# Eight small copies per head pair, from ScalarE to GpSimd

## The chip, the cores and the metric
The kernel runs on one core of a Trainium2 chip. Five engines run their own instruction queues in order and meet through semaphores: TensorE (PE in the profile; its weight loads are PEld), VectorE (DVE), ScalarE (ACT), GpSimd (POOL) and SyncE (SP), which here issues most of the DMAs. The metric is the device time of one execution in microseconds. Before, three runs gave a median of 1098.16 us (1097.16 to 1098.83).

## The reference
Two blocks follow each other. The first is an attention whose scores count only where query and key fall into the same of 64 hash buckets; the second mixes by a Fourier transform, normalizes, and applies a two-layer perceptron. Sizes: batch 4, 8 heads, sequence 768, head size 64, so the model width is 512 and the hidden width 2048.

```python
q_bits = (np.einsum('bhsd,dk->bhsk', q, proj) > 0)        # 6 bits: a bucket per row
mask = q_bucket[:, :, :, None] == k_bucket[:, :, None, :]
scores = np.where(mask, scale * q @ k^T, -1e9)
attn = exp(scores - max); attn = attn / (sum(attn) + 1e-9)
x = (attn @ v) laid out as (B, S, H*D)
mixed = np.real(fft(fft(x, axis=1), axis=2))
u = x + mixed
un = (u - mean(u)) / sqrt(var(u) + 1e-6)
out = u + np.maximum(un @ w_ch1, 0.0) @ w_ch2
```

The copies in question belong to the division by `sum(attn)`.

## The kernel before
**Order of the work.** The 32 heads are taken two at a time: 16 pairs, four for each of the four batches. `attention(b)` (L972) goes through the pairs of a batch; for each pair it makes the transposed scores in six chunks of 128 keys (`scores`, L894), their exponentials on ScalarE (`weights`, L905), the bucket mask on VectorE (`weigh`, L919, two of them a chunk; in the first five pairs the mask is folded into the scores by an extra product, L886), the running sum of the chunks on VectorE (L1007), and the products with the values on TensorE (`values`, L930). Between chunks the generator yields, and the main loop (from L1536) takes steps of `mix(b - 1)` there: the Fourier products of the batch before (`fold` L1072, L1122, L1151, L1165), then its perceptron `mlp7`, whose first layer is written as seven products for each block of hidden units (`inner`, L1426, evacuated by L1448 to L1477) and whose second layer likewise (`outer7`, L1306, evacuated by L1318 to L1358). The statistics for the normalization run in `spread` (L1183 to L1188), the last two instructions of it on GpSimd.

In the first batch, ScalarE and VectorE also turn the raw 64-bit weights into floats (`narrow`, L639 to L655): `weights1` during the attention of batch 0, `weights2` during that of batch 1. The loads of `weights2` (L693) are issued from GpSimd's queue, two raw buffers deep; so are the stores of the first three batches (L1060). L576, L568 and L562 load q, k and v from SP's queue, L768 transposes q and k, L750 takes their norms on ScalarE.

**What sets the order.** The instructions up to the end of batch 0's attention stand in the program's own order on TensorE, VectorE, ScalarE and GpSimd (`tc.manual_schedule`, with L1528 to L1535 at its end). From there on, a scheduler in the compiler's front end places the instructions of each engine by its own estimate of their costs; so a change of one instruction's engine can move others.

**The changed place.** `scale` (L936) finishes a pair. ScalarE moves the two accumulated halves out of PSUM (L941, L944). TensorE sums the exponentials over the partitions by products with ones, each of the four quarters of 32 partitions receiving the sums of one (half, head) (L949). VectorE transposes that in 32 x 32 blocks (L956), so that the 384 sums of a quarter stand as 32 partitions x 12 columns, adds a small constant (L958) and takes the reciprocal, `rc` (L959). There the generator yields once. Then eight copies of 32 partitions x 12 columns lay `rc` out as `rr`, each quarter of `rc` on two quarters of partitions (L965); VectorE transposes `rr` back, each column repeated 32 times (L966), and multiplies the pair's result by it (L970). `rr` has two buffers, `rt` one.

The second transpose waits for all eight copies, and all eight wait for the reciprocal. The other neighbours that the prediction speaks of: L669 and L672, averages of weight rows at the end of batch 0; L839, L843 and L849, the bucket numbers of the later pairs; L1082 to L1100 (`fold`); L1272 to L1275 and L1277, sums of second-layer weights; L1177 and L1178 (`across`), transposes of the normalization's input; L1405 to L1411, sums for `mlp7`; L1325, L1336 and L1339, ScalarE's copies out of PSUM in `outer7`; L1326 and L1334, sums on VectorE there. PSUM tiles of these parts come from pools of two banks, so a product can start only when the evacuation two tiles back is done.

Of the kernel before, what the change touches and what calls it, by code (L numbers as in the profile page):

```python
# [485 lines left out]
def _main(  # L486
# [13 lines left out]
    nc = tc.nc  # L500
# [13 lines left out]
    def wt(shape, dtype, tag, name, bufs=2):  # L514
        return work.tile(shape, dtype, tag=tag, name=name, bufs=bufs)
# [4 lines left out]
    def pt(shape, name):  # L520

        turn[0] += 1
        if roomy[0] and turn[0] % 2:
            if turn[0] % 4 == 1:
                return ps_o.tile(shape, F32, tag="o", name=name)
            return ps_sc.tile(shape, F32, tag="sc", name=name)
        return ps_1.tile(shape, F32, tag="ps", name=name)
# [408 lines left out]
    def scale(n, oos, sums):  # L936


        x = xs[n // NPAIR][:, n % NPAIR]
        vs = wt([P, 1], F32, "vs", f"vs{n}")  # L940
        nc.scalar.copy(vs, oos[0][:, HALF : HALF + 1])  # L941
        halves = [x[:, g * HALF : (g + 1) * HALF] for g in range(2)]
        for g, xg in enumerate(halves):
            nc.scalar.activation(xg, oos[g][:, 0:HALF], AF.Identity, bias=vs)  # L944

        ps = pt([P, HALF], f"sum{n}")
        for i, part in enumerate(sums):
            for j in range(4):
                nc.tensor.matmul(  # L949
                    ps[32 * j : 32 * j + 32, :], ones, part[:, j // 2, j % 2],  # L950
                    start=(i == 0), stop=(i == len(sums) - 1),
                )


        rt = wt([P, S], F32, "rt", f"rt{n}", 1)
        nc.vector.transpose(rt[:, 0:HALF], ps)  # L956
        rc = wt([P, HALF // 32], F32, "rc", f"rc{n}")
        nc.vector.tensor_scalar(rc, rt[:, 0:HALF:32], S * EPS, None, op0=ALU.add)  # L958
        nc.vector.reciprocal(rc, rc)  # L959
        yield  # L960
        rr = wt([P, 2, HALF // 32], F32, "rr", f"rr{n}")
        for g in range(2):
            for i in range(4):
                j = 2 * g + i // 2
                nc.scalar.copy(rr[32 * i : 32 * i + 32, g], rc[32 * j : 32 * j + 32])  # L965
        nc.vector.transpose(  # L966
            rt.rearrange("p (j i) -> p j i", i=32),
            rr.rearrange("p g j -> p (g j)")[:, :, None].broadcast_to([P, S // 32, 32]),
        )
        nc.vector.tensor_tensor(x, x, rt, op=ALU.mult)  # L970

    def attention(b):  # L972
# [3 lines left out]
        def finish():  # L976
            n, c, pk, oos, sums = pending.pop(0)
            with behind() if n >= NPAIR and t is not None else nullcontext():
                values(n, c, pk, oos)
            if c == NT - 1:  # L980
                scales.append(scale(n, oos, sums))
                next(scales[-1])
# [647 lines left out]
```

## Time and profile before
| | |
|---|---|
| median of three runs | 1098.16 us |
| the profiled execution | 1095.54 us, its span 1093.6 us |
| TensorE busy | 1034.4 us (95%) |
| VectorE busy | 788.6 us (72%) |
| ScalarE busy | 499.2 us (46%) |
| GpSimd busy | 58.3 us (5%), 132 instructions |
| TensorE's granted clock, mean | 0.994 |
| DMA | 103.14 MB, 94 GB/s on average |

The span is the time between the first and the last record of one execution. A line of the profile gives start and length in microseconds, the engine, the line of the kernel, the operation, output and inputs by the program's names with their shapes, and a count; in brackets stands how long the engine had been idle before it and what ended that. A group's line gives least, median and greatest duration in nanoseconds. TensorE idles little, and nearly all of its gaps lie in the first 340 us and around 420 to 490 and 680 to 750; the rest of the span it is busy for 19 to 20 of every 20 us.

### The profile page before, as it was taken

What the parts mean: (1) busy time and instruction counts of PE and PEld (TensorE: products, weight loads), DVE (VectorE), ACT (ScalarE), POOL (GpSimd) and SP (SyncE); (2) the same over time, 40 slices, a digit from 0 to 9 for tenths busy, and PEclk for the clock granted to TensorE, in tenths of its full rate; (3) what the DMA queues carried; (4) which work ended last, traced back from release to release, by engine and by line L of the source; (5) the groups of instructions that cost most, each with busy time, mean ns of one, the idle gap of its engine ahead of it and who ended that gap; (6) DMA issues with size and microseconds to landing.
All of it is one profiled execution on the core that took longest, in us unless ns stands there. A gap on an engine that the chain in (4) does not pass through costs nothing.

```text
span 1093.6 us, 14135 instructions
## 1 busy us (share of the span) xinstructions
PE 1034.4 (95%) x4933; PEld 633.6 (58%) x4933; DVE 788.6 (72%) x1336; ACT 499.2 (46%) x1055; POOL 58.3 (5%) x132
## 2 busy tenths in 40 slices
PE   7989897999989999999999999999999999999996
PEld 3333354446744676545664576645675579768675
DVE  5899968868599978694857786876765875644353
ACT  6987556653276324354325424354415522340420
POOL 0000000002000020010000011001000002100000
PEclk9999999999999999999999999999999999999998
DMA  9755352440056162223063224213123205122401
GB/s 233 216 97 126 63 145 67 164 149 11 20 155 207 43 206 40 54 57 84 15 181 85 63 63 159 44 36 91 25 82 113 76 20 173 54 82 84 129 20 42
DMA packets 175711, 103.14 MB, mean 94 GB/s; under 512 B 129552, under 2 KB 162960, under 8 KB 175632
## 3 DMA queue, kind: packets, MB, share of 16 engines
q1 hardware_dynamic: 169840, 88.65, 30.2%
q0 software_dynamic: 4224, 13.11, 3.8%
q8 instruction: 41, 0.67, 0.2%
q10 hardware_dynamic: 1568, 0.39, 0.2%
q14 instruction: 38, 0.31, 0.1%
HBM read 81.14 MB, written 20.97 MB: 93 GB/s over the span
## 4 chain that ended last, share of the span: by engine, by line
PE 57%; DVE 16%; ACT 4%; issue 2%; DMA 2%; DVEq 0%; ACTq 0%
PE o L1306 23%; PE h_p L1426 18%; PE oo L930 5%; PE sc L894 5%; DVE pk L919 5%; DVE acc L1007 3%; PE cs L1122 2%; DMA zraw<-in_moe_w_ch_dram 2%; PE A L1151 1%; PE B L1151 1%; ACT pk L905 1%; ACT rr L965 1%; PE bits L825 1%; DVE x L1165 1%; DVE h L1464 0%
## 5 line engine op out<-in xcount | busy, mean ns | idle before, releaser
L1306 PE MATMUL o<-w,h 128*128 128x256 f32 x1152 | 258.5, 381 | 2.0 <-DVE w L1318 0.8
L1306 PEld LDWEIGHTS o<-w,h 128*128 128x128 f32 x1152 | 216.8, 190 | 41.8 <-issue 3.5
L905 ACT ACTIVATE pk<-sc 128x768 f32<-128x768 f32 x192 | 146.8, 808 | 93.4 <-PE oo L930 30.6
L1426 PE MATMUL h_p<-x,w 128*128 128x384 f32 x448 | 162.4, 492 | 2.2 <-ACT h L1448 1.7
L894 PE MATMUL sc<-qt,kt 64*128 64x384 f32 x768 | 153.5, 502 | 5.9 <-ACT pk L905 5.6
L930 PE MATMUL oo<-pk,vn 128*64 128x385 f32 (+1 forms) x768 | 149.2, 499 | 6.8 <-DVE pk L919 4.4
L919 DVE SCALAR_TENSOR_TENSOR pk<-qb,kb,pk 128x768 f32<-128x768 bf16 x132 | 129.1, 1010 | 34.3 <-ACT pk L905 34.0
L1426 PEld LDWEIGHTS h_p<-x,w 128*128 128x128 f32 x448 | 82.5, 190 | 67.1 <-issue 6.5
L1007 DVE TENSOR_TENSOR acc<-acc,pk 128x1536 f32<-128x1536 f32 (+1 forms) x72 | 105.7, 1482 | 5.7 <-ACT pk L905 5.1
L1426 PE MATMUL h_p<-w 128*128 128x384 f32 x288 | 106.4, 492 | 3.5 <-ACT w L1463 2.3
L930 PEld LDWEIGHTS oo<-pk,vn 128*64 128x64 f32 x768 | 50.7, 136 | 95.0 <-issue 73.3
L894 PEld LDWEIGHTS sc<-qt,kt 64*128 64x128 f32 x768 | 66.4, 186 | 56.8 <-ACT pk L905 19.1
L1426 PEld LDWEIGHTS h_p<-w 128*128 128x128 f32 x288 | 53.0, 190 | 45.5 <-ACT w L1475 5.1
L1318 DVE SCALAR_TENSOR_TENSOR w<-o,rs,w 128x256 f32<-128x256 f32 x56 | 26.7, 477 | 42.4 <-PE o L1306 42.4
L1336 ACT COPY tq<-o 128x256 f32<-128x256 f32 x24 | 8.9, 372 | 101.8 <-PE o L1306 101.8
L1306 PE MATMUL o<-w 128*128 128x256 f32 x176 | 42.0, 381 | 0.3 <-DVE w L1318 0.3
L1459 DVE TENSOR_TENSOR h<-h 128x384 f32<-128x384 f32 x32 | 17.7, 552 | 29.5 <-ACT h L1458 29.5
L1452 DVE TENSOR_TENSOR h<-h 128x384 f32<-128x384 f32 x32 | 17.7, 553 | 26.8 <-ACT h L1451 26.7
L1306 PEld LDWEIGHTS o<-w 128*128 128x128 f32 x176 | 33.0, 190 | 6.8 <-issue 1.1
L1060 POOL DMA_DIRECT2D out_dram<-w x30 | 16.4, 548 | 376.4 <-ACT tq L1336 146.2
L1325 ACT COPY tq<-o 128x256 f32<-128x256 f32 x24 | 8.9, 369 | 58.4 <-PE o L1306 58.3
L1122 PE MATMUL cs<-ch,z 128*128 128x128 f32 (+3 forms) x192 | 31.7, 317 | 3.0 <-DVE bt L829 1.9
(170 smaller groups left out, 1311.4 us busy)
## 6 DMA issues: line engine op xcount, KB each, us to landing
w<-ad SPq DMA_DIRECT2D x168, 128.0 KB, 2.0
w<-bd SPq DMA_DIRECT2D x42, 512.0 KB, 4.5
zraw<-in_moe_w_ch_dram POOLq DMA_DIRECT2D x16, 512.0 KB, 4.0
bd<-w SPq DMA_DIRECT2D x14, 512.0 KB, 4.2
vn<-in_v_dram SPq DMA_DIRECT2D x32, 192.0 KB, 3.4
qn<-in_q_dram SPq DMA_DIRECT2D x120, 48.0 KB, 2.3
kn<-in_k_dram SPq DMA_DIRECT2D x60, 96.0 KB, 3.1
zraw<-in_moe_w_ch_dram SPq DMA_DIRECT2D x8, 512.0 KB, 5.9
```

The lines of the kernel that those rows point to most:

```text
L894: last[0] = nc.tensor.matmul(ps[:, h, 0:HALF], kt[rows, ks], qt[rows, qs], start=kb is not None, stop=True,)
L905: nc.scalar.activation(pk[:, g, :, 0:HALF], ps[:, :, 0:HALF], AF.Exp, scale=SCALE)
L919: nc.vector.scalar_tensor_tensor(w, qb[:, h].rearrange("p (g s) -> p g s", g=2), kb[:, h, c : c + 1], w, op0=ALU.is_equal, op1=ALU.mult,)
L930: oo = nc.tensor.matmul(oos[g][h * D : (h + 1) * D, 0:w], nat["v", n][:, (2 * c + h) * D : (2 * c + h + 1) * D], pk[:, g, h, 0:w], start=( ...
L1007: nc.vector.tensor_tensor(acc[:, g], (first if c == 1 else acc)[:, g], new[:, g], op=ALU.add,)
L1122: nc.tensor.matmul(ps[:, pc + 2 * lo : pc + 2 * hi - 1 : 2], z[:, cp, pc, par, t * P : (t + 1) * P], ch[:, cp, pc, lo:hi], start=(cp == 0) ...
L1151: nc.tensor.matmul(ps[:, cols], F[:, par, k, t, j * P : (j + 1) * P], sq[:, t, k, cols], start=(t == 0), stop=(t == 1),)
L1306: nc.tensor.matmul(ps, a[:, r], right7[i][:, r], start=start and r == 0, stop=r == HF // 2 - 1, skip_group_check=not start,)
L1318: nc.vector.scalar_tensor_tensor(t[:, cols], src, r, t[:, cols], op0=ALU.mult, op1=ALU.add)
L1426: nc.tensor.matmul(ps, left[:, k], right[i][:, k], start=start and k == 0, stop=k == 1, skip_group_check=not start,)
L1452: nc.vector.tensor_tensor(c21, c12, c21, op=ALU.add)
L1459: nc.vector.tensor_tensor(c22, c21, c22, op=ALU.add)
```

## The change
The eight copies of L965 are issued on GpSimd instead of ScalarE. Shapes, sources, destinations and the instructions before and behind them in the program stay.

```diff
         for g in range(2):
             for i in range(4):
                 j = 2 * g + i // 2
-                nc.scalar.copy(rr[32 * i : 32 * i + 32, g], rc[32 * j : 32 * j + 32])
+                nc.gpsimd.tensor_copy(rr[32 * i : 32 * i + 32, g], rc[32 * j : 32 * j + 32])
         nc.vector.transpose(
             rt.rearrange("p (j i) -> p j i", i=32),
             rr.rearrange("p g j -> p (g j)")[:, :, None].broadcast_to([P, S // 32, 32]),
         )
```

## The prediction
> **What bounds the kernel now.** I read the page's busy shares first, then the group of the eight copies with who waits for it, then TensorE's own idle gaps, then the order of time around each of the 16 pairs. The pairs are numbered 0 to 15 in the order of their copies.
>
> ```profile
> PE 1034.4 (95%) x4933; PEld 633.6 (58%) x4933; DVE 788.6 (72%) x1336; ACT 499.2 (46%) x1055; POOL 58.3 (5%) x132
> ```
> TensorE is busy 1034.4 of 1093.6 us. Only its 59 us of gaps can shrink, and what grows them costs time.
>
> ```profile
> L965 ACT COPY rr<-rc x128: 183/198/202, 42.9 to 898.0; 32x12 f32<-32x12 f32 x128
> ...
>   DVE rt L966: 11.4, 13
> ```
> The copies' line: 128 copies of about 198 ns. VectorE's transpose (L966) stood idle 13 times, 11.4 us in all, until they were done.
>
> ```profile
> 20.00:100.00 80.00, 73.29 (x496) 28.82 (x492) 74.17 (x124) 72.57 (x146) 0.11 (x1) 1.00 0.65 171
> ```
> The stretch with pairs 0 to 2 (columns: PE, PEld, DVE, ACT, POOL busy): ScalarE works 72.57 of 80 us, and VectorE is fuller still, 74.17.
>
> ```profile
> 47.66 0.34 PE L886 MATMUL sc<-qkb 64*128 64x384 bf16 x2 [1.59 <-ACT pk L905]
> 75.48 0.34 PE L886 MATMUL sc<-qkb 64*128 64x384 bf16 x2 [1.94 <-ACT pk L905]
> 324.45 1.56 PE L1426 MATMUL h_p<-x,w 128*128 128x384 f32 x4 [1.53 <-ACT h L1448]
> 385.15 1.99 PE L1306 MATMUL o<-w,h 128*128 128x256 f32 x8 [0.74 <-ACT tq L1325]
> 466.81 1.56 PE L1426 MATMUL h_p<-w 128*128 128x384 f32 x4 [1.14 <-ACT w L1463]
> ```
> TensorE's waits for ScalarE just behind copies (pairs 0, 1, 6, 7, 8): in brackets the idle time and whom it waited for.
>
> **What GpSimd charges.** Before has no GpSimd copy, so its price is bounded.
>
> ```profile
> 1.45 0.12 POOL L603 MEMSET ones<- 128x32 f32 x1
> 1.50 0.10 POOL L605 MEMSET mhalf<- 128x1 f32 x1
> 478.77 0.22 POOL L1187 TENSOR_SCALAR rs<-mv 128x1 f32<-128x1 f32 x1 [68.45 <-DVE mv L1185]
> 951.76 0.51 POOL L1187 TENSOR_SCALAR rs<-mv 128x1 f32<-128x1 f32 x2
> ```
> Fills that read nothing start 0.05 us apart and overlap. An instruction that reads and writes SBUF takes 0.22 alone; two in a row take 0.51, so the second starts about 0.29 after the first. Eight copies then last between 0.22 + 7 x 0.05 = 0.57 and 8 x 0.29 = 2.3 us. I take 8 x 0.22 = 1.76: L1187 is nearest in kind (small, one input read) but each L1187 also waits for a semaphore, which six of the eight copies don't. To this comes 0.09 us from VectorE's end to GpSimd's start (478.68 to 478.77). So 1.85 us against ScalarE's 1.70 (0.05 and 1.65): the new route is slightly longer where VectorE stands idle for it.
>
> Where VectorE does not stand idle, another row matters.
>
> ```profile
> 260.48 1.76 DVE L1007 TENSOR_TENSOR acc<-acc,pk 128x1536 f32<-128x1536 f32 x1
> 260.63 1.69 POOL L1187 TENSOR_SCALAR rs<-mv 128x1 f32<-128x1 f32 x1 [1.07 <-DVE mv L1185]
> ```
> The 0.22 us instruction took 1.69, until a VectorE instruction with two inputs from SBUF ended. A copy that falls beside such a one is held.
>
> The row leaves VectorE unharmed: at 258.11 its two-input L919, behind a held L1187, took the usual 1.01. [...]
>
> **The change, part by part.** It takes 128 copies, 16 x 1.65 = 26 us, off ScalarE, and puts them on GpSimd. No DMA and no byte is added. The built order of the changed kernel shows that instructions move too: VectorE reaches L966 earlier, ahead of two of L1165 (pair 4), L1272, L639, L1273 and L643 (pair 6) and L1326 (pairs 7, 11, 15), which then stand behind the wait.
>
> Queues. SP keeps its transfers; in the changed order only a few neighbours swap (ad writes and reads with q and k loads), which I cost at nothing since the copies issue none; if one that TensorE needs is late, the price is about a landing, 2.0 us (median of w<-ad). On GpSimd the copies stand behind whatever was issued before them. By the times of before, that is done in time for all but two: pair 4 starts at 179.54 behind a raw-weight load issued at 179.01 (ScalarE began at 180.14), pair 7 at 383.23 behind a store (ScalarE: 383.03). What is queued behind them: in pair 5 the L1187 chain, needed only from about 256, and in pair 6 a load that matters.
>
> - **Pairs 0 to 2.** ScalarE is freed of 1.65 three times. TensorE's gaps that this can close are 1.59 and 1.94 (1.65 of it), 3.2 together; the third has no gap behind it. Against it, VectorE runs two-input work between the reciprocal and L966, and one copy slips in at each boundary: nine boundaries in pair 0 (no wait), five in pairs 1 and 2, so three copies are left, 0.66 us of wait against 0.28 and 0. As VectorE is the fuller engine, I take half the gaps less half the new waits: -1.1 (from -3.2 to 0).
> - **Pair 3.** L669 no longer queues behind copies and a 1.10 gap before L672 shrinks; L966 comes 0.15 later and VectorE sets the next gap (1.05 at 130.93). -0.4 (-1.1 to +0.7).
> - **Pair 4.** The 2.63 gap at 184.43 goes, because the exponential is issued ahead of a conversion that waits for a load. But the second L1165 of B ends at 181.3 + 0.9 + 0.43 + 0.87 + 0.43 = 183.9, not 180.54, and the transposes (L1177) wait for it. -0.3 (-1.2 to +0.5).
> - **Pair 5.** ScalarE frees a 0.98 gap, VectorE's second L919 ends within 0.1 of before. 0 (-1.0 to +0.6).
> - **Pair 6.** The dear one.
>
> ```profile
> 319.67 1.67 ACT L965 COPY rr<-rc 32x12 f32<-32x12 f32 x8 [0.21 <-DVE rc L959]
> 320.46 0.53 POOL L693 DMA_DIRECT2D zraw<-in_moe_w_ch_dram  x1 [7.58 <-DVE w L1272]
> 321.57 0.97 DVE L966 STREAM_TRANSPOSE rt<-rr 128x768 f32<-128x768 f32 x1
> 325.00 0.68 ACT L647 ACTIVATE zraw<-zraw 128x512 int32<-128x512 uint32 x1 [0.59 <-DMA zraw<-in_moe_w_ch_dram]
> 325.57 0.47 ACT L1451 COPY h<-h_p 128x384 f32<-128x384 f32 x1
> ```
> Here GpSimd's load, VectorE's L966 and ScalarE's next conversion stand in the order of time. Copies end at 319.92 + 1.76 = 321.7 (the first is held to 319.92 by L652). The load behind them goes out 1.3 later than 320.46, so L647 starts near 326.2, and L1451, behind it on ScalarE, at 327.4 instead of 325.57. TensorE's next product needs the bank that L1451 empties. The gap of 1.53 closes and a larger one opens behind it: +1.8 (+0.6 to +2.4).
> - **Pair 7.** L1325 is freed, the 0.74 gap goes. But copies end at 383.3 + 1.76 = 385.06, and L966, L1326, L970 and L1318 end at 387.8 instead of 387.1; TensorE waits for that bank. +0.7 (-0.4 to +1.3).
> - **Pairs 8 and 12.** The gaps of 1.14 and 1.13 go, but the chain runs through VectorE (L966 466.29 to L1007 479.25 without a break): +0.12 for the copies, up to +0.5 for a statistic (L1183) put ahead of two masks. +0.3 each (-1.15 to +0.85).
> - **Pairs 11 and 15.** L1326 falls behind L966, so the L1318 that empties a bank ends 0.6 later, and TensorE starts right after it now (645.08, then 645.13). +0.6 each (0 to +1.2).
> - **Pairs 9, 10, 13, 14.** L1007 holds the copies for 1.7 us and L966 comes about 1.3 later. TensorE has 20.00 of 20 us of work in 520 to 540 and 780 to 800, and 19.95 in 580 to 600 and 840 to 860: 0; without that cover about 1.4 each, 5.6.
>
> Sum: -1.1 - 0.4 - 0.3 + 0 + 1.8 + 0.7 + 0.6 + 1.2 = +2.5 us. The profiled execution took 1095.54 (span 1093.6 and 1.9 around it), so 1098.0. The median of the runs, 1098.16, lies 2.6 above it; there +2.5 gives 1100.7.
>
> **Rivals.**
> 1. *The copies overlap as the fills do (0.66 us from reciprocal to transpose).* For it: six of eight wait for nothing. Against it: fills read no SBUF, and L1187 shows no overlap. All the low ends: -3.2 - 1.1 - 1.2 - 1.0 + 0.6 - 0.4 - 2.3 + 0 = -8.6, 1089.6. It is faster from about 0.15 us per copy on. This is the rival on the other side.
> 2. *The copies are dear (0.29 each) and nothing is gained in pairs 0 to 2.* High ends: 0 + 0.7 + 0.5 + 0.6 + 2.4 + 1.3 + 1.7 + 2.4 = +9.6, 1107.8; with the cover of pairs 9, 10, 13, 14 gone, 1113.4.
> 3. *Gains and losses cancel:* the weight stretch passes all of -3.2 on while the later terms stay: +0.4, 1098.6.
> That the change moves nothing is excluded: the built order has all 128 copies on GpSimd.
>
> **How the numbers follow.** About 0.2% (2.2 us) is what a measurement here tells from no change. The forecast's case has 40% (slower in 23 of them, same 12, faster 5, as the reordering adds a few us either way), rival 1 24% (faster 20, same 4), rival 2 24% (slower 22, same 2), rival 3 12% (same 8, faster 3, slower 1). Faster 0.28, same 0.26, slower 0.46. The range 1091 to 1110 leaves out the far ends of rivals 1 and 2. The forecast's own range is 1098 to 1104.
>
> **What would show it.** ScalarE's busy time falls to about 473, GpSimd's rises by 20 or more. A copy on GpSimd near 0.22 us and eight in about 1.8; L966's waits, 11.4 now, at 20 or more; the load of pair 6 issued over 1 us after the reciprocal; gaps at 47.66 and 75.48 smaller. I am wrong if eight copies last about 1 us, if VectorE's instructions lengthen beside them, or if the reordered stretch from 116 to 340 shifts by more than these terms.

## The result and the profile after

| | before | after |
|---|---|---|
| median, six runs each | 1099.26 us (1097.16 to 1101.23) | 1107.72 us (1107.07 to 1108.26) |
| ratio on record (that of the two medians is 1.0077) | 1 | 1.0082, 95% interval [1.0067, 1.0097] |
| the profiled execution | 1095.54 us | 1108.26 us |
| ScalarE busy | 499.2 us | 476.2 us |
| GpSimd busy | 58.3 us | 96.3 us |

The change makes the kernel 8.5 us slower. The two profiled executions lie 12.7 us apart, because the profile of before caught one of its quickest runs; this section says where those 12.7 went, and the experiments say how much of it belongs to the change.

The line of busy times on the page of after:

```profile
PE 1039.0 (94%) x4933; PEld 634.0 (57%) x4933; DVE 788.5 (71%) x1336; ACT 476.2 (43%) x927; POOL 96.3 (9%) x260
```

The group of the eight copies in after (count, then least, median and greatest duration in ns, first and last start) with who waited for them, in us and times:

```profile
L965 POOL COPY rr<-rc x128: 184/188/1642, 40.6 to 910.6; 32x12 f32<-32x12 f32 x128
...
  DVE rt L966: 24.4, 15
```

ScalarE is 23 us lighter, as it should be. But one GpSimd copy has a median of 188 ns and a greatest value of 1642, and VectorE's idle time at the transpose L966 grew from 11.4 us in 13 places to 24.4 in 15. TensorE's busy time rose by 4.6 us with the same 4933 matmuls: some of them ran at a lower granted clock (0.992 on average against 0.994, and 0.50 in stretches shown below).

The copies themselves, on GpSimd's timeline of after (start, length, number of copies, and in brackets how long GpSimd had been idle), with the VectorE instruction that begins just before the second group:

```profile
472.07 1.80 POOL L965 COPY rr<-rc 32x12 f32<-32x12 f32 x8 [54.29 <-DVE rc L959]
594.95 3.25 POOL L965 COPY rr<-rc 32x12 f32<-32x12 f32 x8 [59.26 <-DVE rc L959]
594.80 1.74 DVE L1007 TENSOR_TENSOR acc<-pk,pk 128x1536 f32<-128x1536 f32 x1
```

In pair 8 VectorE stands idle and eight copies take 1.80 us. In pair 10 the sum L1007, with two inputs from SBUF, starts 0.15 us before them; they take 3.25, and L1007 its usual 1.74.

TensorE's gaps in after (in brackets the gap and what ended it), pairs 0, 1, 5, 6, 7 and 10 in order; the first two answer the gaps at 47.66 and 75.48 of before, the fourth and fifth those at 324.45 and 385.15:

```profile
58.11 1.45 PE L664 MATMUL ws<-w,ones 128*32 128x512 f32 x8 [2.74 <-DVE qkb L805]
89.39 0.50 PE L886 MATMUL sc<-qkb 64*128 64x384 bf16 x2 [2.37 <-DVE qkb L805]
257.39 2.43 PE L930 MATMUL oo<-pk,vn 128*64 128x385 f32 x8 [2.67 <-DVE pk L919]
333.01 1.56 PE L1426 MATMUL h_p<-bt,tq 128*128 128x384 f32 x4 [2.91 <-ACT h L1451]
394.60 1.99 PE L1306 MATMUL o<-w,w 128*128 128x256 f32 x8 [1.85 <-DVE u L1318]
602.44 1.56 PE L1426 MATMUL h_p<-x,w 128*128 128x384 f32 x4 [1.24 <-ACT h L1448]
```

The gaps behind ScalarE in pairs 0 and 1 (1.59 and 1.94) are gone, as hoped, but each was only the first of two. TensorE next waits for VectorE (L805). In before these second waits were short:

```profile
57.34 1.07 PE L664 MATMUL ws<-w,ones 128*32 128x512 f32 x8 [1.23 <-DVE qkb L805]
86.98 0.34 PE L886 MATMUL sc<-qkb 64*128 64x384 bf16 x2 [0.38 <-DVE qkb L805]
```

They are now 2.74 and 2.37: in both pairs the sum of the two gaps stays about what it was (2.82 and 2.32 before).

The reciprocal L959 marks each pair, so the distance from one reciprocal to the next is a good ruler. The table gives it in us for profiled executions of before, after and three of the experiments below; "pair 5" is the stretch that begins at pair 5's reciprocal.

| pair | before | after | held | split | best |
|---|---|---|---|---|---|
| 0, 1, 2 | 28.81, 24.44, 23.89 | 30.19, 26.03, 24.24 | 28.83, 24.47, 24.25 | 28.83, 24.06, 24.17 | 30.18, 24.06, 24.10 |
| 3, 4 | 62.26, 68.62 | 62.71, 68.76 | 62.42, 69.38 | 62.75, 68.23 | 61.78, 65.94 |
| 5 | 71.82 | 73.03 | 71.81 | 71.96 | 71.95 |
| 6 | 63.36 | 64.10 | 63.62 | 66.65 | 63.17 |
| 7 | 81.55 | 82.39 | 81.55 | 81.56 | 81.57 |
| 8 | 59.55 | 60.36 | 59.55 | 58.57 | 58.57 |
| 9 | 62.51 | 62.52 | 62.51 | 62.51 | 62.51 |
| 10 | 54.36 | 55.59 | 55.58 | 54.93 | 54.36 |
| 11 | 81.56 | 82.64 | 81.61 | 81.46 | 81.47 |
| 12 | 59.56 | 60.37 | 59.55 | 58.57 | 58.57 |
| 13 | 61.46 | 61.46 | 61.47 | 61.46 | 61.46 |
| 14 | 52.90 | 53.93 | 53.91 | 52.99 | 52.91 |

From pair 5 to 14 after loses 1.21 + 0.74 + 0.84 + 0.81 + 0.01 + 1.23 + 1.08 + 0.81 + 0 + 1.03 = 7.8 us. Pairs 7 to 14 repeat from run to run within 0.05 us wherever the copies are placed alike. The early stretches don't repeat: in five profiles whose copies in pairs 3 and 4 are as before, those two together took 130.9 to 133.9 us, and the first reciprocal of a run came between 39.6 and 43.6 us. In the two profiles of before and after, the first five pairs (3.9), the start (0.8) and the end (0.3) give the other 4.9 us.

### The profile page after: what moved, and what is told of

Same layout as the page of the kernel before. It is cut to its first block, busy times and chain, and to the rows that moved or that the text cites. A ratio compares the mean times of both kernels' runs of the same rounds, so it can differ in the third digit from the quotient of the medians.

```text
span 1106.3 us, 14148 instructions
## 1 busy us (share of the span) xinstructions
PE 1039.0 (94%) x4933; PEld 634.0 (57%) x4933; DVE 788.5 (71%) x1336; ACT 476.2 (43%) x927; POOL 96.3 (9%) x260
## 5 line engine op out<-in xcount | busy, mean ns | idle before, releaser
L894 PE MATMUL sc<-qt,kt 64*128 64x384 f32 x768 | 156.3, 511 | 2.4 <-ACT pk L905 2.0
L930 PE MATMUL oo<-pk,vn 128*64 128x385 f32 (+1 forms) x768 | 149.1, 497 | 9.5 <-DVE pk L919 7.1
L919 DVE SCALAR_TENSOR_TENSOR pk<-qb,kb,pk 128x768 f32<-128x768 bf16 x132 | 129.0, 1012 | 31.8 <-ACT pk L905 31.1
L1007 DVE TENSOR_TENSOR acc<-acc,pk 128x1536 f32<-128x1536 f32 (+1 forms) x72 | 105.8, 1484 | 6.8 <-ACT pk L905 6.2
L930 PEld LDWEIGHTS oo<-pk,vn 128*64 128x64 f32 x768 | 50.5, 136 | 99.5 <-issue 73.3
L965 POOL COPY rr<-rc 32x12 f32<-32x12 f32 x128 | 34.3, 268 | 444.5 <-DVE rc L959 407.8
L1318 DVE SCALAR_TENSOR_TENSOR w<-o,rs,w 128x256 f32<-128x256 f32 x56 | 26.7, 479 | 43.3 <-PE o L1306 43.3
L1352 DVE TENSOR_TENSOR tq<-tq,o 128x256 f32<-128x256 f32 x24 | 10.0, 418 | 33.8 <-PE o L1306 33.8
```

What stands on the lines that cost most here:

```text
L894: last[0] = nc.tensor.matmul(ps[:, h, 0:HALF], kt[rows, ks], qt[rows, qs], start=kb is not None, stop=True,)
L919: nc.vector.scalar_tensor_tensor(w, qb[:, h].rearrange("p (g s) -> p g s", g=2), kb[:, h, c : c + 1], w, op0=ALU.is_equal, op1=ALU.mult,)
L930: oo = nc.tensor.matmul(oos[g][h * D : (h + 1) * D, 0:w], nat["v", n][:, (2 * c + h) * D : (2 * c + h + 1) * D], pk[:, g, h, 0:w], start=( ...
L965: nc.gpsimd.tensor_copy(rr[32 * i : 32 * i + 32, g], rc[32 * j : 32 * j + 32])
L1007: nc.vector.tensor_tensor(acc[:, g], (first if c == 1 else acc)[:, g], new[:, g], op=ALU.add,)
L1318: nc.vector.scalar_tensor_tensor(t[:, cols], src, r, t[:, cols], op0=ALU.mult, op1=ALU.add)
```

## The experiments

### Early pairs or later ones

Four kernels ask which pairs pay. In `early`, GpSimd makes the copies of pairs 0 to 2 only, in `late` those of pairs 3 to 15 only. `earlyfill` is `early` with some work for TensorE put into the stretch where it waits for VectorE: one small product (L801, the bucket bits of k) is computed three times over for pairs 2 and 3, each time into the same place. `again` is the kernel before once more, as a control.

```diff
-                nc.gpsimd.tensor_copy(rr[32 * i : 32 * i + 32, g], rc[32 * j : 32 * j + 32])
+                if n < 3:        # early, earlyfill;   late: n >= 3
+                    nc.gpsimd.tensor_copy(rr[32 * i : 32 * i + 32, g], rc[32 * j : 32 * j + 32])
+                else:
+                    nc.scalar.copy(rr[32 * i : 32 * i + 32, g], rc[32 * j : 32 * j + 32])
...
-                for j in range(4):
+                for j in [*range(4)] * (3 if io and n in (2, 3) else 1):   # earlyfill, L799
```

> Only pairs 0 to 2 copy on GpSimd; every other instruction stands where it stood before, on every engine. Theory A (the clock): ScalarE, freed, closes TensorE's waits of 1.59 and 1.94 us, but VectorE is the fuller engine there, so the same idle time gathers into one gap of over 2 us ahead of L664 and one ahead of L886 of the next pair, behind which the granted clock falls to about 0.7 for 4 us; the time grows by 2 to 4 us. Theory B (my prediction's term): the gaps close and the time falls by about 1 us. Theory C (only VectorE's waits at L966 count): 0.3 to 0.8 us longer.

> Pairs 0 to 2 copy on ScalarE as before, pairs 3 to 15 on GpSimd, in the order of the changed kernel. Theory A: what the changed kernel loses less the 2 to 4 us of the early stretch, so 5 to 7 us longer than before. Theory B or C: the whole loss, 8 us or more, is here. The waits at L966 should sum to about 23 us.

> As the run with pairs 0 to 2 on GpSimd, but the bucket product of k (L801) for pairs 2 and 3 is computed three times over into the same bank, which puts 1.7 us of work into the two gaps and changes no value. Theory A: both gaps stay below 1.5 us, the granted clock stays near 1.00 between 56 and 100 us, and the time is 2 to 3 us below the run without the filling, within 1 us of before. Theory C: the filling changes nothing or costs up to 1 us.

> The kernel before once more, as a control of the clock: if the dips behind long gaps are a matter of the schedule, the granted clock between 56 and 100 us is 1.00 again and the gaps at 47 and 75 us are 1.6 and 1.9 us again; if they fall at random, a dip may stand there too.

Measured against a median of 1097.93 us before: `early` 1100.73 (ratio 1.0036, [1.0021, 1.0051]), `late` 1109.3 (1.0107, [1.0084, 1.013]), `earlyfill` 1100.84 (1.0029, [1.0014, 1.0045]), and `again` 1098.6. So most of the loss belongs to pairs 3 to 15, and a smaller part to the first three. `early`, 2.8 us longer, lies where theory A put it; `late`, 11.4 us longer, lies above A's 5 to 7, in the range of B and C; `earlyfill`, 2.9 us longer, didn't come back to within 1 us of before. `again` has the gaps of 1.56 and 1.96 us in pairs 0 and 1, with the clock at 1.00 there. The two parts add up to 1.0143, more than the 1.0082 of the whole change; that surplus is not explained. A part of it may lie in the base (the six runs of before beside after have a median of 1099.26 us, the 17 to 23 beside the experiments 1097.45 to 1097.93), and the scatter of the start and of pairs 3 and 4 is of the same size.

What happens in the early pairs shows in stretches of 1.7 us cut from the end of TensorE's gap (columns: PE, PEld, DVE, ACT and POOL busy, then the clock granted to TensorE, the DMA share and GB/s). First after, behind the gap that ends at 89.39:

```profile
89.39:91.09 1.70, 1.70 (x8) 1.00 (x10) 1.58 (x6) 0.00 (x0) 0.00 (x0) 0.50 0.00 0
91.09:92.79 1.70, 1.70 (x10) 0.62 (x8) 1.56 (x3) 0.81 (x1) 0.00 (x0) 0.50 0.00 0
92.79:94.49 1.70, 1.70 (x12) 0.57 (x16) 1.38 (x2) 1.62 (x4) 0.00 (x0) 1.00 0.00 0
```

Then `early`, behind its gap of 2.74 us in pair 0:

```profile
58.79:60.49 1.70, 1.70 (x8) 0.20 (x8) 1.67 (x4) 0.00 (x0) 0.00 (x0) 0.50 0.70 119
60.49:62.19 1.70, 1.70 (x12) 0.87 (x10) 1.65 (x4) 1.37 (x3) 0.00 (x0) 0.56 0.00 0
```

And `earlyfill`, where the repeated products left a gap of 1.47:

```profile
57.87:59.57 1.70, 1.70 (x14) 0.62 (x16) 1.67 (x4) 0.57 (x2) 0.00 (x0) 1.00 0.99 150
59.57:61.27 1.70, 1.70 (x12) 0.69 (x10) 1.65 (x4) 1.64 (x4) 0.00 (x0) 1.00 0.01 1
```

In the 3.4 us behind the longer gap TensorE's granted clock was 0.50 and then 0.56, which loses 1.6 us of work. Without that the stretch of pair 0 is 28.82 us, as before, and not 30.04 as in `early`. So by these two runs the lost clock behind the fused gap is what pair 0 pays. Pair 1 of `early` shows the same without any filling: its gap is 2.37 us, as in after, but the clock behind it is 1.00 where it is 0.50 in after, and the stretch is 24.70 us where after has 26.03 (before 24.44). The time of the whole kernel didn't follow, though: `earlyfill` is no quicker than `early` within their intervals. Its profile has the clock at half elsewhere, behind gaps of 2.44 at 112.57 and 3.06 at 184.83 (the mean over the execution is 0.992, in `early` 0.993); the first of these drops before's profile has too, behind a gap of 1.92 (0.57 in the 4 us from 111.24).

### Is it the wait at the transpose?

Theory W says the later pairs pay because VectorE stands at L966 for the longer way over GpSimd; the rival O puts it down to the changed order of instructions. `twice` issues every GpSimd copy two times in a row. `split` gives GpSimd the copies of odd i and leaves the others on ScalarE.

```diff
+                for _ in range(2):                                   # twice
                     nc.gpsimd.tensor_copy(rr[32 * i : 32 * i + 32, g], rc[32 * j : 32 * j + 32])
...
+                if i % 2:                                            # split
                     nc.gpsimd.tensor_copy(rr[32 * i : 32 * i + 32, g], rc[32 * j : 32 * j + 32])
+                else:
+                    nc.scalar.copy(rr[32 * i : 32 * i + 32, g], rc[32 * j : 32 * j + 32])
```

> Each of the eight GpSimd copies is issued twice in a row (the second writes the same values again), so the way from the reciprocal to the transpose gets some 1.8 us longer and nothing is left out. Theory W: the waits at L966 grow from 24.4 by about 16 x 1.8 = 29 us to some 50, and the pairs that already pay (5 to 8, 10 to 12, 14) pay nearly all of it, pairs 9 and 13 a part: 8 x 1.8 = 14 us or more, 1118 to 1132. Rival O: the waits grow but the order stays as it is, so the time moves by less than 5 us: 1107 to 1112.

> Four of the eight copies (odd i) on GpSimd, four on ScalarE, side by side; nothing is left out. Theory W: the way from the reciprocal to the transpose is about 0.95 us instead of 1.85 where both engines are free, shorter than before's 1.70; where VectorE's two-input sums hold GpSimd (pairs 9, 10, 13, 14) it stays at some 2.4. So the stretches of pairs 5 to 8, 11 and 12 lose nothing against before, 10 and 14 a part: 1097 to 1103. Rival O: the time stays at 1104 to 1109, as the copies still stand on GpSimd and the order differs from before in some 300 places.

`twice` took 1148.56 us (ratio 1.0452, [1.0429, 1.0475]), `split` 1096.23 (0.9983, [0.9968, 0.9997]), against 1097.45 before. In `twice`, what ended VectorE's idle time before the transpose (now L967), in us and times, and the dearest of TensorE's gaps, with the clock behind it:

```profile
  POOL rr L966: 54.8, 15
```

```profile
348.50 2.93 PE L1427 MATMUL h_p<-bt,tq 128*128 128x384 f32 x4 [4.90 <-ACT h L1452]
```

```profile
348.50:350.50 2.00, 2.00 (x3) 1.17 (x4) 2.00 (x5) 1.09 (x3) 0.53 (x1) 0.50 0.00 0
350.50:352.50 2.00, 2.00 (x4) 1.01 (x3) 2.00 (x3) 0.48 (x1) 0.00 (x0) 0.50 0.82 240
```

The waits grew by 30.4 us as expected, but the time by 41 over the changed kernel: more than the waits, and above theory W's 1118 to 1132. TensorE's busy time is 1059.2 us against 1039.0, 20 us more for the same matmuls, and the clock goes with it: its mean is 0.969 against 0.992, and 14 of `twice`'s gaps are followed by a stretch at half clock (0.50 in the two above), four in after. The other half is idle time. By the traces TensorE's order is after's throughout; some eight instructions on VectorE and three on ScalarE stand elsewhere, none of them in pairs 9, 10, 13 and 14, whose stretches grow by 3.5, 4.8, 1.1 and 4.9 us. So the kernel is very sensitive to the length of this way, with the order unchanged too, and theory W's sum held nothing for the clock.

`split` is the other direction of the same dose. In pair 8 the wait is 1.04 us, against 1.74 before and 1.89 after:

```profile
470.47 0.98 DVE L969 STREAM_TRANSPOSE rt<-rr 128x768 f32<-128x768 f32 x1 [1.04 <-POOL rr L966]
```

Its stretches of pairs 8 and 12 fall below before's by 1.0 each, pairs 5, 7 and 11 lose no more than 0.15 any longer, and pair 10 loses 0.57 (the transpose is still 0.45 late there, since the four copies on GpSimd are held by L1007). The kernel as a whole came out just below theory W's 1097 to 1103. By the traces VectorE's order in pairs 8 and 12 is after's, instruction by instruction, and in pair 11 after's but for one; the transpose comes 0.85, 0.85 and 0.90 us earlier there, and the stretches are 1.8, 1.8 and 1.2 us shorter. So VectorE's other order alone isn't what costs in these pairs. On ScalarE two or three copies, and on TensorE one group of products, stand elsewhere in pairs 8 and 12, and in pairs 5 to 7 no run held the order fixed: there the wait and the order aren't separated. The one place where `split` is clearly worse than after is pair 6, +3.3 us against before: a gap of 2.90 us, and the clock at half for about 6 us behind it (the first two products there took 1.65 us together), while after's gap of 2.91 in the same place was followed by a clock of 1.00 (four of these products in 1.56 us).

But the order may have its part. In pair 8 the wait grew by only 0.15 us (1.74 to 1.89), while the stretch grew by 0.81. VectorE's timeline shows what else came later. Before, up to the third sum L1007 of the pair, 14.85 us behind the reciprocal at 464.33:

```profile
474.38 0.69 DVE L1183 BATCH_NORM_STATS2 bs<-w 128x6 f32<-128x512 f32 x1
474.99 1.74 DVE L1007 TENSOR_TENSOR acc<-acc,pk 128x1536 f32<-128x1536 f32 x1
...
478.60 0.66 DVE L1183 BATCH_NORM_STATS2 bs<-w 128x6 f32<-128x512 f32 x1
479.18 1.74 DVE L1007 TENSOR_TENSOR acc<-acc,pk 128x1536 f32<-128x1536 f32 x1
```

After, where the same sum comes 15.61 us behind the reciprocal at 471.79:

```profile
477.96 0.69 DVE L1183 BATCH_NORM_STATS2 bs<-w 128x6 f32<-128x512 f32 x1
...
482.64 0.66 DVE L1183 BATCH_NORM_STATS2 bs<-w 128x6 f32<-128x512 f32 x1
483.22 1.74 DVE L1007 TENSOR_TENSOR acc<-acc,pk 128x1536 f32<-128x1536 f32 x1
...
486.82 0.67 DVE L1183 BATCH_NORM_STATS2 bs<-w 128x6 f32<-128x512 f32 x1
487.40 1.74 DVE L1007 TENSOR_TENSOR acc<-acc,pk 128x1536 f32<-128x1536 f32 x1
```

Three statistics stand ahead of the third sum where there were two. Of the 0.76 us, 0.15 are the longer wait and about 0.6 the statistic drawn ahead. That this is what makes the stretch 0.81 longer is argued from the trace; no run isolated the statistic. `split` has the same three statistics, with the third sum 14.76 us behind the reciprocal, and its stretch is the shortest: where the transpose comes early enough, the statistic costs nothing.

### A later transpose, which didn't come later

`delay` keeps GpSimd and asks for the transpose one chunk later in the program, so that VectorE has other work first; `delayact` does the same with ScalarE's copies.

```diff
                 nc.gpsimd.tensor_copy(rr[32 * i : 32 * i + 32, g], rc[32 * j : 32 * j + 32])
+        yield
         nc.vector.transpose(
...
-                    for sc in scales:
-                        next(sc, None)
-                    scales.clear()
+                    scales[:] = [sc for sc in scales if next(sc, 1) is None]
```

> The eight copies stay on GpSimd, but the program asks for the transpose behind them (L966) and the multiplication (L970) one chunk later, so that VectorE has other work in front of them (not in the last pair of a batch, which has no later chunk). Nothing is left out. Theory W (the loss is VectorE standing at L966 for the longer way over GpSimd): the waits at L966, 24.4 us in the changed kernel, fall below 10, and the stretches of pairs 4 to 6, 8 to 10 and 12 to 14 lose their extra time (0.8 to 1.3 each, some 5 us together); what is left is the last pairs (3, 7, 11, 15) and the early pairs: 1100 to 1104. Rival O (the loss comes from the other order of VectorE's instructions, or from GpSimd being occupied, not from the wait): the time stays at 1106 to 1109 though the waits shrink.

> The same later transpose, with the copies on ScalarE as before: the control for the run with the later transpose on GpSimd. Theory W: waits at L966 fall from 11.4 to below 6, and as the kernel before lost little there, it gains 0 to 3 us: 1095 to 1098; the kernel with GpSimd and the later transpose is within 4 us of it. Rival O: this one moves by as much as the later transpose on GpSimd does (order), and the two stay 8 us or more apart.

`delay` took 1110.12 us (ratio 1.0108, [1.0087, 1.0129]), `delayact` 1098.66 (1.0009, [0.9996, 1.0022]). Their waits before the transpose (now L967), `delay` first:

```profile
  POOL rr L965: 20.7, 13
```

```profile
  ACT rr L965: 8.5, 8
```

Most of the waits stayed: the edit clearly did what it was meant to do only in pairs 0 to 2, where the program's own order holds (with ScalarE in pair 6 too). The wait in pair 4 fell as well, but it is 1.29 and 0.41 us in two profiles of before. In the others the scheduler of the front end set the transpose as early as ever (in pair 8 of `delay` it waits 1.88 us, and the stretch is 60.35, as in after). So this pair of runs says nothing about a later transpose in those pairs, and whether it would give the loss back wasn't tried. In pairs 1 and 2, where it did move, `delay` took 24.06 and 23.59 us against after's 26.03 and 24.24, with the clock at 1.00; `early`, without the move and at full clock there too, took 24.70 and 24.23, so the move itself gave 0.6 in each. The two programs differ only in the engine of the copies and lie 11.5 us apart, where after and before lie 8.5 apart.

### Four pairs alone

The prediction costed pairs 9, 10, 13 and 14 at nothing, because TensorE was busy there for 19.95 to 20.00 of every 20 us. `held` puts those pairs alone on GpSimd.

```diff
+                if n in (9, 10, 13, 14):
                     nc.gpsimd.tensor_copy(rr[32 * i : 32 * i + 32, g], rc[32 * j : 32 * j + 32])
+                else:
+                    nc.scalar.copy(rr[32 * i : 32 * i + 32, g], rc[32 * j : 32 * j + 32])
```

> The copies of pairs 9, 10, 13 and 14 alone on GpSimd, all others on ScalarE; nothing is left out. By the changed kernel's trace GpSimd's copies stand there behind VectorE's two-input sum (L1007) and take 3.25 us, and the transpose comes 1.26 us later. Theory H (that delay alone costs, where TensorE has no reserve): the waits of L966 in these pairs rise from some 0.4 to 1.69, the stretches behind pairs 10 and 14 (54.36 and 52.90 us before) grow by 1.2 and 1.0, those behind 9 and 13 by nothing, the others stay: +2.2 us, 1.001 to 1.003 of the kernel before. Rival (these stretches grow in the changed kernel because of what the earlier pairs shifted): no growth, 0.999 to 1.001.

Measured: 1099.87 us against 1097.78, ratio 1.0013 [1.0001, 1.0026]; the waits at L966 in the four pairs are 1.69 or 1.70. By the table above the stretches of pairs 10 and 14 grow by 1.22 and 1.01, those of 9 and 13 by nothing, and all others from pair 5 on stay within 0.3. By the traces the order on TensorE, VectorE, ScalarE and GpSimd is before's. So the held copies cost this by themselves, without any help from earlier pairs or from another order. TensorE's gap in pair 10 of `held`, 1.24 in after:

```profile
596.43 1.56 PE L1429 MATMUL h_p<-x,w 128*128 128x384 f32 x4 [1.22 <-ACT h L1451]
```

Its chain, on VectorE's, ScalarE's and TensorE's timelines of after (the line numbers of `held` are three higher):

```profile
598.24 0.98 DVE L966 STREAM_TRANSPOSE rt<-rr 128x768 f32<-128x768 f32 x1 [1.69 <-POOL rr L965]
...
600.44 0.55 DVE L1464 TENSOR_TENSOR h<-h,w 128x384 f32<-128x384 f32 x1
601.03 0.53 ACT L1465 ACTIVATE h<-h 128x384 f32<-128x384 f32 x1 [1.89 <-DVE h L1464]
601.50 0.52 ACT L1469 ACTIVATE h<-h 128x384 f32<-128x384 f32 x1
601.93 0.46 ACT L1448 COPY h<-h_p 128x384 f32<-128x384 f32 x1
602.44 1.56 PE L1426 MATMUL h_p<-x,w 128*128 128x384 f32 x4 [1.24 <-ACT h L1448]
```

And the end of the same chain in before:

```profile
592.28 0.46 ACT L1448 COPY h<-h_p 128x384 f32<-128x384 f32 x1
593.09 1.45 PE L1426 MATMUL h_p<-x,w 128*128 128x384 f32 x4
```

The transpose isn't what TensorE waits for. L1464 stands behind it on VectorE, ScalarE's L1465 waits for L1464, and L1448, which empties TensorE's bank, is queued behind L1465. In before the bank was empty at 592.74 and used at 593.09: the reserve was 0.35 us, and in `held` the copy that empties it ends 1.37 us later behind the reciprocal. TensorE being busy all the time said nothing of that.

### VectorE's own copies, and a better placement

`vec` gives all eight copies to VectorE, so that no other engine is waited for. `best` shares the copies as `split` does in pairs 0 to 5, 7, 8, 11, 12 and 15, and leaves them to ScalarE alone in the other five, where `split` had gained nothing or lost.

```diff
+                nc.vector.tensor_copy(rr[32 * i : 32 * i + 32, g], rc[32 * j : 32 * j + 32])   # vec
...
+                if i % 2 and n not in (6, 9, 10, 13, 14):                                       # best
                     nc.gpsimd.tensor_copy(rr[32 * i : 32 * i + 32, g], rc[32 * j : 32 * j + 32])
+                else:
+                    nc.scalar.copy(rr[32 * i : 32 * i + 32, g], rc[32 * j : 32 * j + 32])
```

> All eight copies on VectorE, in the same queue as the reciprocal before and the transpose behind them: no other engine is waited for, and nothing is left out. Estimate for one copy: between 0.05 us (the spacing of the fills) and the 0.17 us of the tensor_scalar on 12 columns (L958), so 0.4 to 1.4 for eight. Theory W (the wait at L966 for the longer way is what costs): no wait at L966, and the transpose 0.6 to 1.5 us earlier than before's 1.96 behind the reciprocal in pairs 3, 5, 7, 8, 11, 12 and 15, so gains of some 1 us in 8 and 12 as with four and four; against it VectorE, full in pairs 0 to 2, gets up to 1 us longer in each: 1094 to 1099. Rival: VectorE's 6 to 20 us of more work come through to the end: 1101 or more.

> Four of the eight copies on GpSimd and four on ScalarE in eleven of the pairs; all eight on ScalarE in pairs 6, 9, 10, 13 and 14, where the run with four and four in every pair gained nothing or lost. Nothing is left out. If the stretches are local (each pair's gain or loss stays its own): -1.0 in each of pairs 8 and 12, about -0.4 in the early ones, no loss in 6 and 10: 2 to 3 us below before, 0.997 to 0.9985. If the order of one pair shifts the next, or the clock decides: 0.9985 to 1.001.

`vec` took 1104.55 us (ratio 1.0047, [1.003, 1.0065]), `best` 1092.68 (0.9942, [0.992, 0.9964]), against 1097.78 before. In `vec` eight copies take 1.41 us, and VectorE is busy 807.6 us, 19 more than before; no wait is left at the transpose. The rival's number, 1101 or more, came true. The gap behind VectorE in pair 0 is 3.27 us there, and the granted clock is 0.50 for the 3.4 us behind it:

```profile
60.67 1.93 PE L664 MATMUL ws<-w,ones 128*32 128x512 f32 x8 [3.27 <-DVE qkb L805]
```

The stretches of pairs 0 to 2 lose 3.6, 2.3 and 1.1 us, where VectorE is the full engine, a part of it by the clock; pairs 8 and 12 win 0.55 each.

`best` keeps the 1.0 us in each of pairs 8 and 12 and loses nothing in 6, 10 and 14. It is the fastest of all, some 5 us below the kernel before and 15 below the change, and below both of its expectations. Of those 5 us only the 2 in pairs 8 and 12 are tied to a place that repeats. The profile's other gain (pair 4, 65.94 against 68.62 us) lies where before itself varies: 65.62 in `again`. In `split`, whose copies stand alike in pairs 0 to 5, pair 4 takes 68.23.

## Why the prediction was right or wrong

The forecast was 1100.7 us and slower; it is 1107.7 and slower, inside the range of 1091 to 1110 but above the forecast's own 1098 to 1104. The direction and half of the mechanism held, several terms did not. The sum was +2.5 us and the difference of the medians is 8.5, so that the time lies inside the range is owed to the width of the range.

| term | forecast, us | the two profiles, us |
|---|---|---|
| pairs 0 to 2 | -1.1 | +3.3 |
| pairs 3, 4 | -0.4, -0.3 | +0.45, +0.14 (not repeatable) |
| pair 5 | 0 | +1.21 |
| pair 6 | +1.8 | +0.74 |
| pair 7 | +0.7 | +0.84 |
| pairs 8, 12 | +0.3 each | +0.81 each |
| pairs 9, 13 | 0 | 0.01, 0 |
| pairs 10, 14 | 0 | +1.23, +1.03 |
| pairs 11, 15 | +0.6 each | +1.08, +0.22 |

- **The price of the copies: right.** Eight were put at 1.76 us and take 1.79 to 1.80 where VectorE idles, and the wait at L966 is 0.15 longer than behind ScalarE (1.89 against 1.74), as 1.85 against 1.70 said. That a copy beside a two-input instruction is held was right too (pair 10: 3.25 us), and so was the 1.3 us by which L966 would be late there: 1.15 to 1.37 in `held`. L966's waits were put at 20 or more, and are 24.4.
- **VectorE unharmed: right.** In pair 10 L1007 takes 1.74 us with the copies behind it, as before. A sharper case is pair 1 of after, where one of the copies is under way when L649, with two inputs from SBUF, starts:

```profile
71.86 0.19 POOL L965 COPY rr<-rc 32x12 f32<-32x12 f32 x1
71.90 0.69 DVE L649 CUSTOM_DVE_ANT_0 w<-w,fraw 128x1024 uint16<-128x1024 uint16 x1
```

  L649 starts 1.37 us behind the reciprocal and takes 0.69, both as in before.
- **Pairs 0 to 2: the step "half the gaps" failed.** It counted the gaps that end at ScalarE (1.59 and 1.94) as closable, and didn't add the gap behind VectorE that follows. ScalarE's gap went, and all of its time reappeared at L805. What the prediction had no term for is the clock: in pairs 0 and 1 two gaps fused to one (2.74 and 2.37), and in the 3.4 us behind each the granted clock was 0.50 (58.67 to 62.08 and 89.39 to 92.80), which loses 1.7 us of work. The waits were put at 0.66 us and are 0.55 in pairs 1 and 2. That the copies of pair 0 slip in at boundaries was wrong: beside four L678, whose second input lies in PSUM, all eight took 1.80 us; in pairs 1 and 2 they were held and took 4.03 and 3.95.
- **Pair 5: the step "VectorE's second L919 ends within 0.1 of before" failed.** In the changed order both L919 stand behind the multiplication L970, and the product L930 waits for the second. TensorE's three gaps of 0.98, 0.16 and 0.94 became one of 2.67. With it pairs 3 to 6 moved by 2.5 us, where their terms sum to 1.1: one of the prediction's own signs of being wrong.
- **Pair 6: right mechanism, too high.** The load left GpSimd at 327.41, 2.1 us behind the reciprocal instead of 1.0; L647 and with it L1451 came 1.05 later against the reciprocal, and TensorE's gap is 2.91 where it was 1.53, +1.4. Later gaps of the stretch shrank, and 0.74 is left. A second cause, which the prediction had named (L643 behind the wait) but not costed, ended at the same time. On ScalarE's timeline of after, the conversion ahead of L647 waited for VectorE's L643, which now stands behind the transpose:

```profile
331.30 0.68 ACT L654 ACTIVATE zraw<-zraw 128x512 f32<-128x512 int32 x1 [3.26 <-DVE w L643]
331.93 0.67 ACT L647 ACTIVATE zraw<-zraw 128x512 int32<-128x512 uint32 x1
332.50 0.46 ACT L1451 COPY h<-h_p 128x384 f32<-128x384 f32 x1
```

  L647 begins 4.5 us behind the load's issue, as in before, where it waited for the load; which of the two would have come last without the other wasn't tried.
- **Pairs 8 and 12: mis-sized.** The prediction saw both causes (+0.12, and up to +0.5 for the statistic) and took 0.3; on VectorE both came in full (0.15 and 0.6), and the stretches grew by 0.81.
- **Pairs 10 and 14: the step "0, TensorE has the work to cover it" failed.** TensorE's busy share (19.95 to 20.00 of 20 us) was the reason given, and the price without cover, 1.4 each, was close to the measured 1.2 and 1.0. In pairs 9 and 13 the delay did cost nothing.
- **Pair 7: right; pair 11: right mechanism, too low.** The L1318 that empties the bank comes later as worked out (a gap of 1.85 us in pair 7). Pair 11 costs 1.08 instead of 0.6. Pair 15 can't be told: the end of the kernel from its reciprocal took 196.5 to 197.7 us in the profiles (198.25 in `twice`).

The number of the second rival, 1107.8, is nearly the time measured, but that is luck, as only half of its story is true: nothing was gained in pairs 0 to 2, yet the copies were not dear.

## What to carry to other kernels

When a small step on a cross-engine route is moved to a free engine, compare the two routes where another engine stands idle for them, not the load of the engines: here 23 us off a busy ScalarE didn't pay for a transpose that came 0.15 to 1.4 us later in thirteen of sixteen places, and in pairs 8 and 12, where nothing held them, splitting the eight copies over two engines beat either engine alone. A busy share of 100% is no cover: look for the reserve of the next bank or buffer (0.35 us in pair 10). And before counting a gap as closable, find what the same engine waits for next, because two short gaps may fuse to one that costs the clock as well (in pair 0 gaps of 1.59 and 1.23 us became one of 2.74, with the clock at 0.50 behind it).

## What the runs showed of the hardware that was not expected

TensorE's granted clock fell behind some of its gaps, and not always behind the longest. These are the gaps of 1.9 us or more in the profiles of before and after, with the mean granted clock of the 4 us behind each:

| profile | gap, us | ends at, us | clock behind it |
|---|---|---|---|
| before | 1.92 | 111.24 | 0.57 |
| before | 1.93 | 139.21 | 1.00 |
| before | 1.93 | 173.94 | 1.00 |
| before | 1.94 | 75.48 | 1.00 |
| before | 2.05 | 223.44 | 0.58 |
| before | 2.63 | 184.43 | 1.00 |
| after | 1.90 | 114.96 | 1.00 |
| after | 1.93 | 178.47 | 1.00 |
| after | 1.99 | 228.10 | 0.65 |
| after | 2.31 | 188.79 | 1.00 |
| after | 2.37 | 89.39 | 0.57 |
| after | 2.67 | 257.39 | 1.00 |
| after | 2.69 | 136.67 | 0.57 |
| after | 2.74 | 58.11 | 0.57 |
| after | 2.91 | 333.01 | 1.00 |

The 0.57 behind the gap that ends at 89.39 is a clock of 0.50 from 89.39 to 92.80 and of 1.00 behind that, or 1.7 us of lost work. Two other kernels, with the same work in pair 0, show too that the length alone didn't decide. `split`, behind a gap of 2.09 us:

```profile
58.76:60.46 1.70, 1.70 (x14) 0.62 (x16) 1.66 (x4) 0.56 (x2) 0.00 (x0) 1.00 0.68 111
```

`best`, behind a gap of 2.07:

```profile
58.85:60.55 1.70, 1.70 (x12) 0.79 (x14) 1.67 (x4) 0.53 (x2) 0.00 (x0) 0.75 0.66 110
60.55:62.25 1.70, 1.70 (x8) 0.81 (x6) 1.65 (x4) 1.64 (x4) 0.00 (x0) 0.50 0.00 0
```

What decided was not shown. Equal kernels differ by some us (the runs of before: 1094.2 to 1101.7, at mean granted clocks of 0.995 and 0.989), though how much of that is the clock and how much the start wasn't separated.
